# A Fourier mixing and expert kernel: the order of work from fixed slots to list scheduling over streams

## The chip, the cores and the metric

The kernel runs on one core of one Trainium2 chip. The metric is device time in microseconds (us) of the whole program. TensorE (PE) multiplies, VectorE (DVE) and ScalarE (ACT) move results out of PSUM and do elementwise work, GpSimd (POOL) issues indirect transfers (scatter and gather by row numbers), and SyncE (SP) issues all other transfers, in order, on one queue. Everything is in float32.

## The reference

Two blocks follow each other. The first filters 8 sequences of 2496 tokens with 256 channels in the frequency domain; the second sends each of the 19968 tokens to the one expert of 8 with the highest logit.

```
X = rfft(x, axis=1);  Y = X * (filt_r + 1j * filt_i);  y = irfft(Y, n=2496)     # x: 8 x 2496 x 256
logits = y @ w_gate;  e = argmax(logits);  gate = softmax(logits)[e]             # per token
out = gate * (relu(y @ w1[e]) @ w2[e])                                           # w1: 8 x 256 x 1024, w2: 8 x 1024 x 256
```

## The kernel before

**The transform.** 2496 = 39 x 64, so the Fourier transform and its inverse are four stages of products with small tables, batch by batch. Stage a (`stage_a`, line 336) multiplies x by a 117 x 117 table and stores z. Stage b (line 349) loads z with the other index along the partitions, multiplies by the tables `tbs`, and VectorE multiplies by the filter `ht`. Stage c (lines 371 and 373) goes back and stores u. Stage d (line 394) loads u, multiplies by `tds` and stores y. z, u and y are tensors in DRAM: their layout is turned on the way out and in. A batch goes in 6 chunks of up to 4 slices for stages a and d and in 5 chunks for b and c. After stage d, y is transposed (`turn_y`, line 407), multiplied by `w_gate` (`logits`, line 421) and turned back (`turn_logits`, line 432).

**The routing.** `route` finds each token's expert and its rank within the expert (two products, lines 468 and 469, called rank products below), and scatters token numbers and gates into a table in DRAM, sorted by expert: 22 indirect transfers per batch on POOL (line 510), 30 for the last batch. `tile_map` then makes tiles of 512, 256 or 128 rows of one expert, 65 in all: one of 256 rows after batch 0, one of 512 and five of 256 after batch 1, then only 512 until the last batch, which ends with 256 and 128.

**The experts.** For each tile `listed` loads its list of rows (line 596), `gather` fetches the rows of y (line 612), `weights` loads w1 and w2 of its expert (1 MB each, lines 631 and 627), `turn_x` transposes (line 639), `hidden` computes relu(x w1) (line 646, eight times two products), `result` multiplies by w2 (line 661), scales by the gate and scatters 128 rows to the output (line 667).

**What sets the order.** A planner in Python writes each engine's order out by hand. `slot(k)` mixes stages b and c of batch k, stage a of batch k+1 and stage d of batch k-1 by fixed places within a slot; `STEPS` is all slots one after the other. The loop at the end takes either the next step of `STEPS` or the next piece of expert work, by a credit that `share()` refills, and keeps a clock `now` of TensorE's work. A transform step may be placed as soon as its load has been put in SP's queue (`f[2] in ins`); it doesn't know when the load lands. `more_loads` fills one ring of 8 input buffers (`fin`, tag "in") in the order of the steps; a load of z or u must wait until the last store of its batch has been put in the queue. Stores are put in the queue two steps late by `move` and `flush`. `prefetch` puts list loads, gathers and weights in the queues as buffers allow. Results of stages a, c and d share five buffers (tag "st"), freed when their stores have landed. The tables are loaded between the steps of slot 0.

SP executes its queue in order: an instruction that waits holds up everything behind it.

```
    NIN = 8
    ...
        if may("list", 3):
            i = got["list"]
            listed(i)
            mark("list", max(now[0], rows_at[work[i][3]]) + 5.0)
    ...
            elif f and (not f[2] or f[2] in ins):
```

Of the kernel before, what the change touches and what calls it, by code (L numbers as in the profile page):

```python
# [133 lines left out]
def kernel(  # L134
# [37 lines left out]
    zd = [dram.tile([N2, N1, D], F32, tag=f"z{b % 2}", name="zd") for b in range(B)]  # L172
    ud = [dram.tile([N2, N1, D], F32, tag=f"u{b % 2}", name="ud") for b in range(B)]
# [44 lines left out]
    free = {"v": 0.0, "s": 0.0, "p": 0.0}  # L218
# [27 lines left out]
    def load_filters(c):  # L246
        f0, n = FH[c]
        nc.sync.dma_start(out=tbs[:, f0:f0 + n], in_=tb[:, f0:f0 + n])
        nc.sync.dma_start(out=ht[:, f0:f0 + n], in_=filt[:, f0:f0 + n, :])
        if c == 0:  # L250
            nc.sync.dma_start(out=ht[:, NF:], in_=filt[:, NF:, :])
            nc.sync.dma_start(out=tcs, in_=tcm)

    def load_rest():
        nc.sync.dma_start(out=tds, in_=td)
# [37 lines left out]
    NIN = 8  # L293

    moves, stored = [[], []], set()

    def move(o, i):
        moves[1].append(lambda: nc.sync.dma_start(out=o, in_=i))

    def mark(key):  # L300
        moves[1].append(lambda: stored.add(key))
# [6 lines left out]

    def fin(key):
        ins[key] = sb.tile([P, 4, D], F32, tag="in", name="fin", bufs=NIN)  # L310
        return ins[key]

    def load_x(b, c):
        i0, n = CH[c]
        nc.sync.dma_start(out=fin(("x", b, c))[:, :n], in_=x[b, :, i0:i0 + n, :])

    def load_z(b, c):
        f0, n = FH[c]
        z0 = 1 if f0 == 0 else 0
        zi = fin(("z", b, c))  # L320
        nc.sync.dma_start(out=zi[:HP, :n], in_=zd[b][:, f0:f0 + n, :])
        nc.sync.dma_start(out=zi[HP:, z0:n], in_=zd[b][:, NF - 1 + f0 + z0:NF - 1 + f0 + n, :])

    def load_u(b, c):
        i0, n = CH[c]
        ui = fin(("u", b, c))
        for r, m, v in columns(ud[b], i0, n):
            nc.sync.dma_start(out=ui[r, :m], in_=v)

    def stage_a(b, c):  # L330
        i0, n = CH[c]
        xt = ins.pop(("x", b, c))
        zo = sb.tile([TP, 4, D], F32, tag="st", name="zo", bufs=5)
# [4 lines left out]
        for r, m, v in columns(zd[b], i0, n):  # L338
            move(v, zo[r, :m])
# [3 lines left out]
    def stage_b(b, f):  # L343
# [16 lines left out]
        free["v"] = max(free["v"], now[0]) + 2.8  # L360

    def stage_c(b, f):
        ys = outs.pop(("y", b, f))
        j = f % 4
        if j == 0:
            outs["u", b] = sb.tile([P, 4, D], F32, tag="st", name="uo", bufs=5)
# [8 lines left out]
        if j == 2:  # L375
            f0 = f - 2
            z0 = 1 if f0 == 0 else 0
            move(ud[b][:, f0:f0 + 4, :], uo[:HP])
            move(ud[b][:, NF - 1 + f0 + z0:NF - 1 + f0 + 4, :], uo[HP:, z0:])
# [3 lines left out]
    def stage_d(b, c):  # L383
# [4 lines left out]
        yo = outs["o", b, c] = sb.tile([TP, 4, D], F32, tag="st", name="yo", bufs=5)  # L388
# [9 lines left out]
        for r, m, v in columns(ytok, i0, n):  # L398
            move(v, yo[r, :m])
# [39 lines left out]
    def route(b):  # L439
# [68 lines left out]
        rows_at[b] = pool(now[0] + 5.0, len(rows)) + 3.0  # L508
# [124 lines left out]
    def turn_x(i):  # L633
        n, xg = work[i][0], xgs.pop(i)
        xts[i] = moe.tile([P, DH, 4 * P], F32, tag="xT", name="xT")
# [17 lines left out]
    def result(i, j):  # L653
# [10 lines left out]
        pool(now[0], 1)  # L664
        either(D, lambda: nc.vector.tensor_scalar(ys, in0=p[:, :D], scalar1=gate, scalar2=None, op0=ALU.mult),  # L665
# [13 lines left out]
    def slot(k):  # L679

        steps, nch = [], len(CH)
        if k < B:
            for f in range(0, NF + 2, 2):
                at = f / (NF + 2)
                if f < NF:
                    steps.append((at, lambda f=f: stage_b(k, f), ("z", k, f // 4) if f % 4 == 0 else None, 0.85))
                if f >= 2:
                    steps.append((at + 0.01, lambda f=f: stage_c(k, f - 2), None, 0.85))
        if k + 1 < B:
            for c in range(nch):  # L690
                steps.append((0.7 * c / nch, lambda c=c: stage_a(k + 1, c), ("x", k + 1, c), 0.43 * CH[c][1]))
        if k > 0:
            for c in range(nch + 3):
                at = 0.2 + 0.8 * c / (nch + 3)
                if c < nch:
                    steps.append((at, lambda c=c: stage_d(k - 1, c), ("u", k - 1, c), 0.43 * CH[c][1]))
                if c >= 3 and c % 2:
                    steps.append((at + 0.01, lambda c=c: logits(k - 1, (c - 3) // 2), None, 0.9))
                if 1 <= c <= nch:
                    steps.append((at + 0.03, lambda c=c: turn_y(k - 1, c - 1), None, 0.22 * CH[c - 1][1]))  # L700
                if c >= 3 and c % 2:
                    steps.append((at + 0.04, lambda c=c: turn_logits(k - 1), None, 0.25))
            steps.append((2.0, lambda: begin_route(k - 1), None, 0.0))
        return sorted(steps, key=lambda step: step[0])

    STEPS = []
    for c in range(len(CH)):
        STEPS.append((0.0, lambda c=c: stage_a(0, c), ("x", 0, c), 0.43 * CH[c][1]))
        if c < len(FH):
            STEPS.append((0.0, lambda c=c: load_filters(c), None, 0.0))  # L710
    STEPS.append((0.0, load_rest, None, 0.0))
    SLOT = []
    for k in range(B + 1):
        steps = slot(k)
        SLOT.append(sum(step[3] for step in steps))
        STEPS += steps

    def begin_route(b):
        flush(True)
        sides.append(after(b))  # L720
        left_t[0] = SLOT[b + 2] if b + 2 <= B else 1.0


# [144 lines left out]
```

## Time and profile before

| | |
|---|---|
| median of 3 runs | 1713.04 us (1707.46 to 1716.94) |
| profiled execution, its own time | 1714.15 us |
| its span, first to last instruction | 1712.4 us |
| mean granted clock of TensorE | 0.960 |
| instructions | 20473 |
| bytes moved by DMA | 296.11 MB, mean 173 GB/s |
| DMA packets | 120962 |

Busy time by group of instructions (count, busy us, mean ns of one record; a float32 product shows as two records):

| group | count | busy us | mean ns |
|---|---|---|---|
| result, line 661, w2t | 2240 | 501.3 | 381 |
| hidden, line 646, all forms | 2080 | 589.5 | 436 |
| result, line 661, w2s | 368 | 83.2 | 379 |
| stage b, line 349, all forms | 320 | 92.3 | 412 |
| stage d, line 394, all forms | 352 | 92.1 | 403 |
| stage a, line 336 | 176 | 89.1 | 631 |
| stage c, line 373 | 144 | 79.1 | 633 |
| scatter to the table, line 510 (POOL) | 176 | 174.2 | 990 |
| scatter to the output, line 667 (POOL) | 163 | 163.2 | 1001 |
| gather, line 612 (POOL) | 163 | 157.6 | 967 |

How to read it: the span is one execution as the hardware profiler saw it; the medians are from runs of their own. Matmuls are pipelined and the profile models their ends, so the mean of one record is longer than the distance from one to the next. In a row by stretch the columns are the stretch, its length, the busy us of PE, PEld (weight loads), DVE, ACT and POOL with counts, the granted clock, the busy share of the 16 DMA engines and the GB/s moved. In a list of waits, "PE bank L432 <- ACT yt L232: 33.1, 2, 17.9" says that TensorE's line 432 waited for ScalarE's line 232, 33.1 us in total, twice, at most 17.9. In order of time the bracket at the end is the engine's idle time before the row and what ended it; SPq is SP's queue, and its rows are the issue of a transfer. Line 232 is `evac`, the helper for all copies out of PSUM; line 298 is `move`, for all stores.

### The profile page before, as it was taken

How to read it: one execution, taken by the hardware profiler on the slowest of the kernel's cores; microseconds unless marked ns; L12 is line 12 of the kernel's file. 1: busy time of each engine (PE TensorE's matmuls, PEld its weight loads, DVE VectorE, ACT ScalarE, POOL GpSimd, SP SyncE). 2: the span in 40 equal slices, each digit the busy share in tenths (PEclk: the TensorE clock that was granted, in tenths of full speed). 3: DMA queues.
4: the chain of work that ended last, by engine and by line, in shares of the span. 5: the costliest groups of instructions: out<-in, count | busy, mean ns of one | idle time of the engine just before them, and what ended most of it. 6: DMA issues, size and time to landing. Idle time of an engine off the chain costs nothing. (4 is left out here: it accounts for less than half of the span.)

```text
span 1712.4 us, 20473 instructions
## 1 busy us (share of the span) xinstructions
PE 1574.1 (92%) x6822; PEld 1123.0 (66%) x6822; DVE 561.3 (33%) x1355; ACT 321.6 (19%) x587; POOL 504.5 (29%) x526
## 2 busy tenths in 40 slices
PE   2888387898999999999999989999999999999997
PEld 1454245577857766666657657666666668889996
DVE  0647173354452214322252223231000003334442
ACT  1233131311232122222222212221212120000000
POOL 0002315024234311531234315374322222222221
PEclk7889688999999999999999999999999999999999
DMA  8988787658876354664365343405343435554551
GB/s 293 274 250 207 209 232 199 209 174 215 276 198 216 129 180 130 161 217 138 112 154 172 117 135 104 160 5 194 131 163 136 155 132 201 184 184 173 175 185 41
DMA packets 120962, 296.11 MB, mean 173 GB/s; under 512 B 32338, under 2 KB 73028, under 8 KB 105893
## 3 DMA queue, kind: packets, MB, share of 16 engines
q1 hardware_dynamic: 99322, 252.77, 48.4%
q0 software_dynamic: 21536, 42.03, 7.5%
q8 instruction: 56, 0.92, 0.2%
q14 instruction: 48, 0.39, 0.1%
HBM read 212.74 MB, written 82.88 MB: 173 GB/s over the span
## 5 line engine op out<-in xcount | busy, mean ns | idle before, releaser
L646 PE MATMUL bank<-xT,w1t 128*128 128x512 f32 (+2 forms) x2080 | 589.5, 436 | 6.7 <-DVE xT L232 5.0
L661 PE MATMUL bank<-w2t,hT 128*128 128x256 f32 x2240 | 501.3, 381 | 4.6 <-DVE hT L649 4.6
L646 PEld LDWEIGHTS bank<-xT,w1t 128*128 128x128 f32 x2080 | 340.8, 192 | 215.8 <-issue 188.3
L661 PEld LDWEIGHTS bank<-w2t,hT 128*128 128x128 f32 x2240 | 421.7, 191 | 71.0 <-issue 10.8
L667 POOL DMA_INDIRECT out_dram<-ys,idt x163 | 163.2, 1001 | 570.6 <-DVE ys L665 193.4
L510 POOL DMA_INDIRECT table<-pay,row x176 | 174.2, 990 | 318.9 <-DVE row L495 216.5
L612 POOL DMA_INDIRECT xg<-yd,idt x163 | 157.6, 967 | 306.4 <-PE bank L639 234.1
L665 DVE TENSOR_SCALAR ys<-bank,idt 128x256 f32<-128x256 f32 x151 | 73.0, 484 | 476.5 <-PE bank L661 431.3
L650 ACT ACTIVATE hT<-bank 128x512 f32<-128x512 f32 (+1 forms) x234 | 137.4, 587 | 476.1 <-PE bank L646 476.1
L649 DVE TENSOR_SCALAR hT<-bank 128x128 f32<-128x128 f32 (+1 forms) x286 | 96.9, 339 | 70.1 <-PE bank L646 68.1
L349 PE MATMUL bank<-fin,tbs 128*128 128x256 f32 (+1 forms) x320 | 92.3, 412 | 27.4 <-issue 26.3
L394 PE MATMUL bank<-fin,tds 117*117 117x256 f32 (+1 forms) x352 | 92.1, 403 | 17.2 <-DMA fin<-ud 16.6
L349 PEld LDWEIGHTS bank<-fin,tbs 128*128 128x128 f32 (+1 forms) x320 | 62.3, 206 | 59.7 <-issue 47.5
L394 PEld LDWEIGHTS bank<-fin,tds 117*117 117x117 f32 (+1 forms) x352 | 66.5, 193 | 49.0 <-issue 23.9
L336 PE MATMUL bank<-fin,tas 117*117 117x512 f32 x176 | 89.1, 631 | 6.3 <-DMA fin<-in_x_dram 5.8
L356 DVE TENSOR_TENSOR ys<-bank,ht 128x512 f32<-128x512 f32 x80 | 55.1, 688 | 117.7 <-PE bank L349 117.5
L373 PE MATMUL bank<-ys,tcs 128*128 128x512 f32 x144 | 79.1, 633 | 12.1 <-DVE ys L359 6.2
L232 ACT COPY xT<-bank 128x512 f32<-128x512 f32 (+2 forms) x69 | 29.4, 432 | 305.4 <-PE bank L639 201.4
L232 ACT COPY uo<-bank 128x512 f32<-128x512 f32 x80 | 46.9, 586 | 201.4 <-PE bank L373 120.0
L232 DVE COPY xT<-bank 128x512 f32<-128x512 f32 (+2 forms) x61 | 29.1, 477 | 165.2 <-PE bank L639 165.0
L661 PE MATMUL bank<-w2s,hT 128*128 x368 | 83.2, 379 | 0.0
L661 PEld LDWEIGHTS bank<-w2s,hT 128*128 128x128 f32 x368 | 68.1, 190 | 8.3
(103 smaller groups left out, 769.0 us busy)
## 6 DMA issues: line engine op xcount, KB each, us to landing
w1t<-in_moe_w_dram SPq DMA_DIRECT2D x65, 1024.0 KB
w2t<-in_moe_w_dram SPq DMA_DIRECT2D x42, 1024.0 KB
fin<-in_x_dram SPq DMA_DIRECT2D x40, 512.0 KB
zd<-zo SPq DMA_DIRECT2D x120, 156.0 KB
fin<-ud SPq DMA_DIRECT2D x120, 156.0 KB
yd<-yo SPq DMA_DIRECT2D x120, 156.0 KB
fin<-zd SPq DMA_DIRECT2D x72, 256.0 KB
ud<-uo SPq DMA_DIRECT2D x72, 256.0 KB
```

Source lines behind the costliest of these rows:

```text
L232: either(n, lambda: nc.vector.tensor_copy(o, i), lambda: nc.scalar.copy(out=o, in_=i))
L336: mm(p[:TP, :], lhsT=tas, rhs=xt[:TP, j:j + 2, :], start=True, stop=True)
L349: mm(p[:, i * D:(i + 1) * D], lhsT=tbs[:k, f + i, :], rhs=zi[:k, j + i, :], start=True, stop=True)
L373: mm(p, lhsT=tcs[:, 1, :], rhs=ys, start=True, stop=True)
L394: mm(p[:TP, i * D:(i + 1) * D], lhsT=tds[:k, i0 + j + i, :], rhs=ui[:k, j + i, :], start=True, stop=True)
L510: sc = nc.gpsimd.indirect_dma_start(out=table, out_offset=bass.IndirectOffsetOnAxis(ap=at, axis=0), in_=what, in_offset=None,)
L612: nc.gpsimd.indirect_dma_start(out=xgs[i][:, j], out_offset=None, in_=yd[0:rows, :], in_offset=bass.IndirectOffsetOnAxis(ap=idt[i].bitcast ...
L646: mm(p[:, :m], lhsT=w1t[i][:, dh, k * P:(k + 1) * P], rhs=xts[i][:, dh, :m], start=(dh == 0), stop=(dh == DH - 1))
L649: either(m, lambda: nc.vector.tensor_scalar_max(hT[:, :m], p[:, :m], 0.0), lambda: nc.scalar.activation(hT[:, :m], p[:, :m], AF.Relu))
L650: lambda: nc.scalar.activation(hT[:, :m], p[:, :m], AF.Relu))
L661: mm(p[:, :D], lhsT=hs[i][k][:, j * P:(j + 1) * P], rhs=w2, start=(k == 0), stop=(k == FT - 1))
L667: nc.gpsimd.indirect_dma_start(out=out, out_offset=bass.IndirectOffsetOnAxis(ap=ids.bitcast(U32)[:, j, 0:1], axis=0), in_=ys, in_offset=No ...
```

## The change

The order by slots goes. There are now four streams, each with its own order: A (stage a), X (stages b and c), Y (stage d, transposes, logits, routing) and the experts. `transform()` takes the first step of Y, X or A, in this priority, whose input has landed by the planner's clock; A may run one batch ahead of X. The planner keeps a time for the transfers (`free["d"]`, at 240 or 380 GB/s by kind) and `ready` times of loads and of VectorE's results. A list load is put in SP's queue only when the planner's clock has passed the batch's scatters. Input buffers are per stream (2 for x, 3 for z, 3 for u), z and u have a DRAM tensor for each batch, "st" has six buffers, the transposed expert input one. The tables come with the z loads of batch 0, each part ahead of its chunk. `share()` counts what is left of the streams up to the next routing. What is computed stays the same.

```
-    zd = [dram.tile([N2, N1, D], F32, tag=f"z{b % 2}", name="zd") for b in range(B)]
+    zd = [dram.tile([N2, N1, D], F32, tag=f"z{b}", name="zd") for b in range(B)]
...
+    ROW, ROWS = 0.24e6, 0.38e6
+    def dma(size, rate):
+        free["d"] = max(free["d"], now[0]) + size / rate
+        return free["d"] + 2.5
...  load_filters: the filters' last part by chunk
+        half, f1 = divmod(f0, NF // 2)
+        rows = slice(half * HP, (half + 1) * HP)
+        nh = min(n, NF // 2 - f1)
+        nc.sync.dma_start(out=ht[rows, NF + f1:NF + f1 + nh], in_=filt[rows, NF + f1:NF + f1 + nh, :])
+        if nh < n:
+            nc.sync.dma_start(out=ht[HP:, NF:NF + n - nh], in_=filt[HP:, NF:NF + n - nh, :])
         if c == 0:
-            nc.sync.dma_start(out=ht[:, NF:], in_=filt[:, NF:, :])
             nc.sync.dma_start(out=tcs, in_=tcm)
...
-    NIN = 8
+    NIN = {"x": 2, "z": 3, "u": 3}
...
     def mark(key):
-        moves[1].append(lambda: stored.add(key))
+        def store():
+            stored[key] = free["d"] + 2.0
+        moves[1].append(store)
...  load_z
+        if b == 0:
+            load_filters(c)
+            if c == 2:
+                load_rest()
...  load_x, load_z, load_u return when the load lands
+        return dma(P * n * D * 4, ROWS)        # x and z
+        return dma(TP * n * D * 4, ROW)        # u
...
-        zo = sb.tile([TP, 4, D], F32, tag="st", name="zo", bufs=5)
+        zo = sb.tile([TP, 4, D], F32, tag="st", name="zo", bufs=6)
...
-        rows_at[b] = pool(now[0] + 5.0, len(rows)) + 3.0
+        rows_at[b] = pool(now[0] + 1.0, len(rows)) + 3.0
...
-        xts[i] = moe.tile([P, DH, 4 * P], F32, tag="xT", name="xT")
+        xts[i] = moe.tile([P, DH, 4 * P], F32, tag="xT", name="xT", bufs=1)
...  slot() and STEPS go; A, X and Y hold (batch, step, cost, input)
+    def more_loads():
+        for kind, load, todo, source in loads:
+            while todo and sum(key[0] == kind for key in ins) < NIN[kind]:
+                b, c = todo[0]
+                if source and stored.get((source, b), 1e9) > now[0]:
+                    break
+                todo.pop(0)
+                ready[kind, b, c] = load(b, c)
+    def transform():
+        for stream in (Y, X, A):
+            if stream and (not stream[0][3] or ready.get(stream[0][3], 1e9) <= now[0]):
+                if stream is A and stream[0][0] > (X[0][0] + 1 if X else B):
+                    continue
+                return stream
+        return None
...  prefetch
-        if may("list", 3):
-            i = got["list"]
-            listed(i)
-            mark("list", max(now[0], rows_at[work[i][3]]) + 5.0)
+        if may("list", 3) and rows_at[work[got["list"]][3]] <= now[0]:
+            listed(got["list"])
+            mark("list", now[0] + 5.0)
...  share
-        return min(4.0, max(0.3, (known - RESERVE) / max(left_t[0], 1.0)))
+        return min(4.0, max(0.3, (known - (45.0 if b < B - 1 else 80.0)) / max(left, 1.0)))
...  the loop
+            f = transform()
+            asked = e and when.get(e[2], 1e9) <= now[0]
+            if asked and (credit > 0.0 or not f):
                 e[0]()
                 now[0] += e[1]
-                credit -= e[1]
+                credit = max(credit - e[1], -20.0)
...
+            elif f:
+                step = f.pop(0)
+                step[1]()
+                now[0] += step[2]
+                credit = min(credit + share() * step[2], 20.0)
             else:
-                now[0] += 1.0
+                now[0] += 0.5
```

## The prediction

> **What bounds the kernel now.** I read the page's busy lines and slices first, then busy time by stretch, then TensorE's waits in the first 323 us, then SP's own waits, then the order of time around one long wait.
>
> ```profile
> PE 1574.1 (92%) x6822; PEld 1123.0 (66%) x6822; DVE 561.3 (33%) x1355; ACT 321.6 (19%) x587; POOL 504.5 (29%) x526
> ...
> PEclk7889688999999999999999999999999999999999
> DMA  8988787658876354664365343405343435554551
> ```
> ```profile
> 0.00:250.00 250.00, 166.76 (x600) 96.58 (x600) 119.92 (x233) 64.28 (x117) 28.53 (x43) 0.83 0.84 244
> 250.00:323.00 73.00, 51.24 (x244) 36.42 (x244) 34.64 (x88) 14.39 (x28) 26.83 (x28) 0.86 0.75 211
> 323.00:420.00 97.00, 90.09 (x373) 66.69 (x367) 39.65 (x101) 18.24 (x35) 35.68 (x36) 0.96 0.69 185
> 420.00:1167.00 747.00, 732.84 (x2999) 496.85 (x2998) 237.13 (x572) 169.48 (x298) 268.07 (x273) 0.99 0.53 157
> 1167.00:1712.00 545.00, 533.12 (x2616) 426.43 (x2614) 129.93 (x364) 55.16 (x110) 145.34 (x148) 0.99 0.44 155
> ```
> Columns: stretch, length, busy us of PE, PEld, DVE, ACT, POOL, granted clock, DMA share, GB/s. From 323 us on TensorE is the bound: it idles 7 + 14 + 12 us in 1389. Before 323 it idles 105 of 323 us and runs at 0.83 to 0.86 of its clock while the DMA share is 0.84: this stretch is bound by transfers.
>
> ```profile
> PE bank L432 <- ACT yt L232: 33.1, 2, 17.9
> PE bank L349 <- issue: 26.3, 1, 26.3
> PE bank L394 <- DMA fin<-ud: 10.8, 3, 6.5
> ...
> SPq L596 <- DMA table<-pay,row: 17.8, 2, 10.8
> ```
> ```profile
> 181.92 0.47 SPq L322 DMA_DIRECT2D fin<-zd  x1
> 190.96 0.38 SPq L596 DMA_DIRECT2D idt<-table  x1
> 192.15 0.82 SPq L631 DMA_DIRECT2D w1t<-in_moe_w_dram  x1
> 193.76 0.34 SPq L627 DMA_DIRECT2D w2t<-in_moe_w_dram  x1
> 194.21 1.31 SPq L298 DMA_DIRECT2D zd<-zo  x3
> ...
> 210.65 0.69 DVE L232 COPY yo<-bank 117x512 f32<-117x512 f32 x1 [20.08 <-DMA zd<-zo]
> ...
> 211.79 0.53 PE L432 MATMUL bank<-ident,ls 128*117 128x128 f32 x1 [17.90 <-ACT yt L232]
> ```
> The third block is TensorE's waits up to 323 us (total, times, longest) with one of SP's; the last is order of time. SP has one in-order queue. At 182 us it reaches the list load of batch 0, which needs all 22 scatters of that batch, and stands 8.6 us (a second time 265.4 to 277.6: 12.2). Behind it wait the stores that free the "st" buffers, so VectorE and ScalarE cannot evacuate, and TensorE stops for 17.9 and 15.2 us. The 26.3 us wait is the first z load behind 6.5 MB of tables.
>
> **The unit of the sum.** I add up TensorE's work at full clock. A product of 512 columns takes two records of 0.43 us (32 records of L646 fill 13.73 us), one of 256 columns 0.43 us in all (64 records of L661: 13.82 us), eight transposes of y 0.80, eight logit products 0.93. All work of the program is then 1518 us. It is the same in both programs; only its order differs. The landmark is the start of the first 512-row expert tile, from which on TensorE has expert work to fill gaps with. Before, it starts at 323.2 us (the transposes of line 639). By the built order, 183 us of work stand before it: 55 products of stage a (47.3), 80 of b (34.4), 43 of c (33.5), 66 of d (28.4), transposes and logits 20.8, the 256-row tile and the small rest 18.4. So 140 us are lost by then. From there to the last product's end at 1701.6 are 1378.4 us for 1335.3 of work: 43 lost (22.6 idle by the stretches above, the rest clock and rounding). After it 10.8 us of last store and end. 183 + 140 + 1335 + 43 + 11 = 1712, the span. The profiled execution took 1714.15, the median is 1713.04: I subtract 1.1 at the end.
>
> **The change, part by part.**
>
> *List scheduling.* In the changed program's order the same landmark has 54, 72, 38 and 66 products of stages a to d before it, 175 us of work. Rank products of batch 1 come after 122 us of work instead of 128, of batch 2 after 165 instead of 230, since batches no longer go in lockstep slots. But transfers bound this stretch, so I count bytes in SP's queue. Up to the landmark tile's w1 load: 65.6 MB before, 67.2 MB after. The order alone does not lighten the start: fewer z and x loads of later batches, but the same tables and stores.
>
> *The list load's gate.* `listed` is now put in the queue only when the planner's clock has passed the last scatter (22 x 1.3 us planned, 1.29 measured start to start). The two blocks, 20.8 us of a standing queue, go. In the early stretch the planner's rates (240 and 380 GB/s) are above the 244 measured, so real time runs behind the planner and the scatters have longer than planned: the gate should hold. What is late next: the 2 MB of weights themselves, which still go ahead of the stores (7 us at 290 GB/s).
>
> *When the landmark comes.* Two workings. (a) The w1 load of the landmark was issued at 278.8 us; less 20.8 of standing queue 258; 1.6 MB more at 260 GB/s, 6; landing 5 (the u load issued at 88.98 us was used at 94.16): 269. (b) 67.2 MB at 260 GB/s (the share-1 rate is 244/0.84 = 290; I take a share of 0.90, between 0.84 and the 0.97 to 1.04 of the best 10 us pieces), 258, and 5: 263. I take 266. Bounds: 67.2/0.244 + 5 = 280, and at a share of 0.97, 67.2/0.281 + 5 = 244.
>
> *Tables with the z loads.* The 6.5 MB of tables move from between the stores of batch 0 to behind them. The filters' last quarter comes in pieces, which adds 5 DMAs to SP's queue (about 0.45 us each, L251's issue), 2 us on a queue that is waiting for bytes anyway: 0. What was late before (z0 at 43.5 us) is late still, for table bytes come directly ahead of each z chunk. It is inside the bytes above.
>
> *Own z and u tensors per batch, own buffers per stream.* Removes waits on old loads and stores (SP's waits on zd and ud before a load are 1 to 3 us each). Eight shared input buffers become 2 for x, 3 for z, 3 for u: look-ahead gets shorter. After the landmark some 70 loads (30 u, 22 z, 18 x) remain, and each is issued only when the step that used its buffer is done. The planner gives a u load 0.479 MB/240 + 2.5 = 4.5 us; the trace shows 5.2 in the busy start. z: 3.9 planned, 3.75 shown (39.76 to 43.51). If every u, z and x load were late by 0.7 us, that is 49 us. Against it: before, steps were placed as soon as their load was issued, with no landing time, and after 323 us TensorE waited for inputs from ud once, 5.8 us. Expert products stand between most steps. I take 5 us. Bounds: -20 (all 22.6 us of late idle gone but what the rank products cause) and +49.
> [...] The measurement decides on the latency; how much of it is covered only the run tells.
>
> *st 5 to 6, xT 2 to 1.* One more store buffer loosens the evacuations (gain inside the above). With one xT the transposes of tile i+1 still come after all products that read xT of tile i on the same engine: 0; where they cannot go early, the evacuation is exposed once, at most the 5.0 us that the first tile shows (PE L646 after DVE xT L232).
>
> *The end.* The last batch's first tile comes 66 us of work after its rank products (10.4 + 13.8 + 0.9 + 3 x 13.8). Before, from those (1109.83) to the list load (1154.71) took 44.9; 3.6 for the list (190.96 to 194.60), 4.8 for four gathers, 4.3 for landing (first x load: 1.32 to 5.58): 57.6. Covered by 9 us: I take 0. If it slips: up to 10 us.
>
> Sum: 266 + 1343 (1518 - 175) + 43 + 5 + 10.8 = 1667.8, plus 1.75 around the span, less 1.1: **1668 us**.
>
> **Rivals.**
> *A. The queue runs nearly full* and the late idle goes too. Landmark 244, late term -15 instead of +5: 1668 - 22 - 20 = 1626. For: pieces of 10 us at a share of 1.0. Against: the pieces between them at 0.65, where SP waits for evacuations; that dependency stays.
> *B. The gate does not hold or bytes bind harder.* Landmark 280 and 0.2 us per load: 1668 + 14 + 9 = 1691. If SP blocks as before, the 33.1 us of TensorE's wait come back: 1701. For: 1.6 MB more in the queue than before.
> *C. Slower: short look-ahead.* Every load after the landmark becomes a bubble on the in-order TensorE. From 1663 without bubbles, 70 loads x 0.71 us reach 1713; at 1 us each, 1733. For: 2 x buffers, and the 5.2 us above. Against: the one late wait before, and that DMA share is 0.53 there.
>
> **How the numbers follow.** Half a per cent, 8.6 us, is about what can be told from no change. Forecast 0.52 (1645 to 1690), A 0.14, B 0.17 (three quarters of it faster, the rest no change), C 0.17 (0.03 of it within half a per cent). Faster 0.52 + 0.14 + 0.13 = 0.79; same 0.04 + 0.03 = 0.07; slower 0.14. The range 1626 to 1722 leaves out the best of A and most of C. If the change is faster at all, 1626 to 1701.
>
> **What would show it.** The first 512-row tile near 266 us (A: 244, B: 280); no SP wait on table scatters before it and no TensorE wait over 10 us on ScalarE's yt; the DMA share to that point near 0.90. In the later stretch, TensorE's idle near 25 us with waits on fin<-ud, fin<-zd or fin<-in_x under 10 us in sum (C: 50 or more, in many waits of about 1 us). Rank products of the last batch to its first tile without a gap over 5 us. The forecast falls if the queue stands for evacuations instead of lists, or if TensorE's order was planned for transfers faster than they are.

## The result and the profile after

The changed kernel takes 1762.31 us (median of 4 runs, 1751.32 to 1765.67) against 1713.78 for the kernel before: a ratio of 1.0277, 95% interval 1.0223 to 1.033. It is slower; the prediction said 1668. The profiled execution has a span of 1760.4 us and took 1762.14. The runs below were taken in groups, each beside the kernel before, which took 1711 to 1718 us in three groups, 1793 in that of e5 to e8 and 1796 in that of e17 and e18, so between groups only ratios are compared.

The page of the changed kernel, busy line and slices:

```profile
PE 1596.1 (91%) x6822; PEld 1127.9 (64%) x6822; DVE 568.6 (32%) x1369; ACT 315.6 (18%) x573; POOL 505.6 (29%) x526
...
PE   5587877499899999989999999999988999999997
...
DMA  7998869548535842374483643473243435555551
```

Busy time by stretch, columns as before (stretch, length, PE, PEld, DVE, ACT, POOL, granted clock, DMA share, GB/s). The second stretch ends at the landmark of the prediction, the start of the first 512-row expert tile:

```profile
0.00:250.00 250.00, 173.13 (x594) 97.82 (x595) 122.96 (x273) 56.28 (x102) 35.36 (x50) 0.84 0.87 233
250.00:333.00 83.00, 46.97 (x230) 31.96 (x228) 36.14 (x88) 14.00 (x25) 39.42 (x41) 0.82 0.81 213
333.00:420.00 87.00, 85.55 (x339) 63.65 (x340) 25.26 (x47) 15.07 (x30) 18.22 (x19) 0.95 0.50 154
420.00:1167.00 747.00, 718.29 (x2829) 478.47 (x2829) 228.79 (x493) 166.78 (x292) 238.89 (x242) 0.98 0.52 158
1167.00:1760.00 593.00, 572.19 (x2835) 455.99 (x2833) 155.50 (x469) 63.49 (x125) 173.74 (x176) 0.98 0.43 149
```

The landmark comes at 333 us: ten later than before, 67 later than predicted. In the 250 to 333 stretch TensorE works 47 of 83 us. The late stretches are worse too: 28.7 us idle in the fourth where the kernel before had 14.2.

TensorE's waits over the whole span (total, times, longest):

```profile
PE bank L669 <- DMA xg<-yd,idt: 48.7, 16, 30.0
PE bank L365 <- DMA fin<-in_x_dram: 26.2, 10, 7.0
PE bank L378 <- DMA fin<-zd: 25.9, 6, 8.8
...
PE bank L676 <- DVE xT L239: 10.1, 1, 10.1
...
PE bank L424 <- DMA fin<-ud: 4.0, 5, 1.8
```

The 33.1 us of waits on ScalarE's yt, which the change was to remove, are gone. New are one wait of 30.0 us for gathered rows (`turn_x`, now line 669), one of 10.1 us for a copy, and many smaller ones for x (line 365), z (line 378) and gathered rows. Where the 30 us come from shows in order of time, by the queues of SP and POOL and by TensorE:

```profile
290.15 0.38 SPq L626 DMA_DIRECT2D idt<-table  x1
291.33 0.37 SPq L661 DMA_DIRECT2D w1t<-in_moe_w_dram  x1
...
273.20 1.02 POOL L698 DMA_INDIRECT out_dram<-ys,idt  x1 [6.04 <-issue]
299.08 1.01 POOL L540 DMA_INDIRECT table<-pay,row  x1 [24.86 <-DVE row L525]
...
327.00 0.90 POOL L540 DMA_INDIRECT table<-pay,row  x1 [0.30 <-issue]
328.45 0.98 POOL L642 DMA_INDIRECT xg<-yd,idt  x1 [0.55 <-DMA table<-pay,row]
...
301.99 1.02 PE L403 MATMUL bank<-ys,tcs 128*128 128x512 f32 x2
333.05 0.75 PE L669 MATMUL bank<-ident,xg 128*128 128x128 f32 x2 [30.04 <-DMA xg<-yd,idt]
```

The tile's list is loaded at 290. POOL is idle from 274 to 299, but the next instruction in its queue is the first of batch 2's 22 scatters (line 540), and it waits 24.86 us for its row numbers. Then all 22 go, one each 1.29 us, and only at 328.45 the first gather (line 642). The tile comes next in TensorE's written order, so TensorE stands from 303 on.

The 10.1 us stand at the last batch, in order of time on VectorE and TensorE:

```profile
1311.54 0.48 DVE L696 TENSOR_SCALAR ys<-bank,idt 128x256 f32<-128x256 f32 x1 [25.64 <-DMA out_dram<-ys,idt]
...
1324.60 0.68 DVE L239 COPY xT<-bank 128x512 f32<-128x512 f32 x1
...
1314.15 1.13 PE L676 MATMUL bank<-xT,w1t 128*128 128x512 f32 x2 [0.28 <-ACT xT L239]
1325.33 16.04 PE L676 MATMUL bank<-xT,w1t 128*128 128x512 f32 x30 [10.05 <-DVE xT L239]
```

POOL's queue in the same place, the last scatter to the table and the first two to the output:

```profile
1294.34 0.97 POOL L540 DMA_INDIRECT table<-fill,pad  x1 [0.30 <-issue]
...
1305.58 1.03 POOL L698 DMA_INDIRECT out_dram<-ys,idt  x1 [0.30 <-issue]
...
1312.25 1.03 POOL L698 DMA_INDIRECT out_dram<-ys,idt  x1 [4.38 <-DVE ys L696]
```

The 30 scatters of the last batch hold POOL's queue until 1295; then it stands 6.46 us at a gather, and only at 1305.58 does the next scatter to the output go. Until then the four ys buffers stay full, and VectorE stands 25.64 us on a free one. After that the outputs follow 3 to 7 us apart, each with one ys result of VectorE behind it. The copy that TensorE needs is the next but three on VectorE.

Here the stall cost somewhat more than its length. The same place by stretches of 5 us (the columns as above; the clock is the one after POOL's):

```profile
1310.00:1315.00 5.00, 4.72 (x24) 3.46 (x22) 0.48 (x1) 0.59 (x1) 1.03 (x1) 1.00 1.04 416
1315.00:1320.00 5.00, 0.28 (x1) 0.00 (x0) 0.48 (x1) 0.00 (x0) 1.01 (x1) 0.75 0.76 309
1320.00:1325.00 5.00, 0.00 (x0) 0.00 (x0) 1.28 (x3) 0.00 (x0) 2.74 (x3) 0.50 0.21 67
1325.00:1330.00 5.00, 4.67 (x6) 2.09 (x7) 0.28 (x1) 0.60 (x1) 3.11 (x4) 0.50 0.38 116
1330.00:1335.00 5.00, 5.00 (x11) 2.15 (x11) 0.00 (x0) 1.59 (x3) 1.53 (x2) 0.88 0.07 26
```

After the stall TensorE still has half its clock for some 6 us (to about 1331), which by an estimate from these rows costs 3 us: the stall of 10.05 us is worth some 13. By an estimate from the same rows, the mean of 0.75 puts the fall from 1.00 to 0.50 some 2 to 2.5 us after the last product (1315.3), and the mean of 0.88 puts the return some 6 us after the work (1325.3).

By the prediction's unit (TensorE's work at full clock, 1518 us in all) the loss up to the landmark and behind it is:

| kernel | span | landmark | work before it | lost before it | lost after it |
|---|---|---|---|---|---|
| before | 1712.4 | 323.2 | 182.9 | 140 | 54 |
| after | 1760.4 | 333.1 | 175.3 | 158 | 84 |
| e1, gather first | 1731.0 | 298.9 | 175.3 | 124 | 89 |
| e2, gate alone | 1706.9 | 304.0 | 182.9 | 121 | 68 |
| e4, 4/2/2 buffers | 1697.1 | 330.7 | 194.2 | 136 | 43 |
| e9, e1 once more | 1728.8 | 296.4 | 175.3 | 121 | 90 |
| e10, 8 ys, 5 st | 1728.0 | 314.5 | 175.3 | 139 | 71 |
| e11, 2 xT, 5 st | 1746.3 | 313.3 | 175.3 | 138 | 90 |
| e13, 3/3/2 buffers | 1675.4 | 300.8 | 183.9 | 117 | 40 |
| e14, 2/3/2 buffers | 1716.6 | 358.1 | 194.2 | 164 | 35 |

Lost before is the landmark less the work before it; lost after is the span less the landmark less the rest of the work. "After it" holds the 10.8 us of the last stores. Of the 48 us between before and after, 18 lie before the landmark and 30 behind it.

### The profile page after: what moved, and what is told of

It reads as the page before. It is cut to its first block, busy times and chain, and to the rows that moved or that the text cites. A ratio compares the mean times of both kernels' runs of the same rounds, so it can differ in the third digit from the quotient of the medians.

```text
span 1760.4 us, 20409 instructions
## 1 busy us (share of the span) xinstructions
PE 1596.1 (91%) x6822; PEld 1127.9 (64%) x6822; DVE 568.6 (32%) x1369; ACT 315.6 (18%) x573; POOL 505.6 (29%) x526
## 5 line engine op out<-in xcount | busy, mean ns | idle before, releaser
L676 PE MATMUL bank<-xT,w1t 128*128 128x512 f32 (+2 forms) x2080 | 599.4, 441 | 14.1 <-DVE xT L239 10.1
L696 DVE TENSOR_SCALAR ys<-bank,idt 128x256 f32<-128x256 f32 x142 | 68.6, 483 | 466.2 <-PE bank L691 424.7
L365 PE MATMUL bank<-fin,tas 117*117 117x512 f32 x176 | 100.5, 704 | 26.2 <-DMA fin<-in_x_dram 26.2
L669 PE MATMUL bank<-ident,xg 128*128 128x128 f32 x326 | 53.4, 291 | 48.7 <-DMA xg<-yd,idt 48.7
L239 DVE COPY xT<-bank 128x512 f32<-128x512 f32 (+2 forms) x63 | 30.2, 479 | 191.9 <-PE bank L669 191.6
L424 PE MATMUL bank<-fin,tds 117*117 117x256 f32 (+1 forms) x352 | 85.7, 382 | 5.4 <-DMA fin<-ud 4.0
L669 PEld LDWEIGHTS bank<-ident,xg 128*128 128x128 f32 x326 | 41.4, 148 | 67.8 <-issue 47.5
L365 PEld LDWEIGHTS bank<-fin,tas 117*117 117x117 f32 x176 | 36.3, 214 | 73.6 <-issue 61.6
```

The lines of the kernel that those rows point to most:

```text
L365: mm(p[:TP, :], lhsT=tas, rhs=xt[:TP, j:j + 2, :], start=True, stop=True)
L424: mm(p[:TP, i * D:(i + 1) * D], lhsT=tds[:k, i0 + j + i, :], rhs=ui[:k, j + i, :], start=True, stop=True)
L669: nc.tensor.transpose(pt[:, j, :], xg[:, j, dh * P:(dh + 1) * P], ident)
L676: mm(p[:, :m], lhsT=w1t[i][:, dh, k * P:(k + 1) * P], rhs=xts[i][:, dh, :m], start=(dh == 0), stop=(dh == DH - 1))
```

## The experiments

Line numbers in an experiment's rows are those of its own kernel. Theory: POOL's queue works in order, so the gather stood behind scatters (30 us); two x buffers slow the start; the tail's output buffers cost 10 us and a half-clock stretch. Rivals: bytes bind the start, the rows come late by themselves, or what one place gains another takes back.

### e1 and e9: the gather ahead of the scatters

```
+            if b == HELD:                     # HELD = 2: kept back until the next gather() is in the queue
+                held.append(lambda at=at, what=what: scatter(at, what))
...
-            gather(i)
+            name = gather(i)
+            if len(rows_at) > HELD:
+                let_go(name)                  # each held scatter is ordered behind that gather
```

> The changed kernel with one thing moved: the 22 table scatters of batch 2 are queued on GpSimd behind the gather of the first 512-row expert tile and not ahead of it; the orders of TensorE and of the load queue are as in the changed kernel. Theory (GpSimd's queue works in order, and the gather stood behind scatters that waited 24.86 us for their row numbers and then took 28 us): the list of that tile is issued at 290, its rows can be gathered from 295 and land by about 303, and TensorE's work before it ends at 303.0; the wait of 30.04 us at that tile falls to 0 to 4 us, the tile starts at 302 to 307 and the kernel takes 1732 to 1740. Rival one (the rows come late for the transfer's own sake, behind other traffic): the wait stays above 20 us and the time within 1755 to 1768. Rival two (what is gained at the tile is lost again later, because the late part is bound by something else): the tile starts near 305 but the time stays above 1750.

Measured: 1731.65 us, ratio 1.0134 (1.0102 to 1.0167). POOL and TensorE in order of time:

```profile
290.33 0.99 POOL L656 DMA_INDIRECT xg<-yd,idt  x1 [20.14 <-DMA idt<-table]
...
309.19 1.02 POOL L548 DMA_INDIRECT table<-pay,row  x1 [0.31 <-issue]
...
298.85 0.59 PE L684 MATMUL bank<-ident,xg 128*128 128x128 f32 x2
```

The gather runs as soon as its list has landed, and the tile starts at 298.9 without a wait, somewhat ahead of the expected 302 to 307. The time falls by 30.7 us, as much as the wait was long, but the two kernels were timed in different groups: by ratio (1.0277 and 1.0134) it is 25 us, and against e3, which has the same wait (30.2 us) and ran beside e1, it is 21. The first theory holds; both rivals fall. The loss before the landmark is now 124, less than before the change; the loss behind it hardly moves (84 and 89).

> The kernel with the gather put first once more, to stand beside the next three on one chip. Theory and rivals as before: a ratio of 1.008 to 1.019 to the kernel before, a stall of 10 to 12 us at the last batch's second dense tile (TensorE waiting for VectorE's xT copy).

The same kernel in another group: 1731.51 us, ratio 1.0104 (1.0048 to 1.016).

### e2: the gate alone, in the kernel before

```
-        if may("list", 3):
+        if may("list", 3) and rows_at[work[got["list"]][3]] <= now[0]:
```

> The kernel before with one part of the change alone: a list is loaded only when the planner reckons its scatters done. Theory (of the prediction): the load queue no longer stands on lists ahead of landmark tile and the 33.1 us for which TensorE waited on token transposes there go for the most part; first 512-row tile at 295 to 305 in place of 323, time 1688 to 1700. Rival (the queue stood where the transfers were behind anyway, or the gated list is then late for the tile itself): the waits move to gathered rows or to loads of x, z and u, the first 512-row tile stays within 315 to 330, time 1705 to 1725.

Measured: 1710.37 us, ratio 0.9999 (0.9962 to 1.0036). TensorE in order of time:

```profile
240.09 3.73 PE L394 MATMUL bank<-fin,tds 117*117 117x256 f32 x8 [11.56 <-DMA fin<-ud]
...
303.97 1.09 PE L639 MATMUL bank<-ident,xg 128*128 128x128 f32 x8
```

The waits on yt vanish and the landmark comes at 304, as expected; but 11.6 us of a u load and others take part of their place, the next tile (327.6) is only 10.7 us earlier than before (338.3), and the span 5.5 us shorter. In the time of the runs nothing is left. So the 20.8 us of a standing load queue, which the prediction took as the gain in its working (a), were worth at most 6 us in the kernel before.

### e12: the changed kernel without the gate

```
-        if may("list", 3) and rows_at[work[got["list"]][3]] <= now[0]:
-            listed(got["list"])
-            mark("list", now[0] + 5.0)
+        if may("list", 3):
+            i = got["list"]
+            listed(i)
+            mark("list", max(now[0], rows_at[work[i][3]]) + 5.0)
```

> The kernel with the gather put first, and without the gate on the lists: a list is loaded as soon as a buffer is free, as before. The planner's order shifts a little with it. Theory (the gate makes the first list of each batch late, and the 17 us of waits on gathered rows after 350 us with their half-clock stretches are its price): these waits fall below 6 us and the ratio is 0.006 to 0.014 lower. Rival (without the gate the load queue stands on scatters, as in the kernel before with 8.6 and 12.2 us): TensorE waits on token transposes or loads come back, ratio the same within 0.003 or higher.

Measured: 1781.12 us, ratio 1.0383 (1.0325 to 1.0442), 50 us above e9. One line of SP's waits and TensorE's two largest, in order of time:

```profile
SPq L640 <- DMA table<-pay,row: 149.4, 16, 32.0
```
```profile
192.97 3.73 PE L365 MATMUL bank<-fin,tas 117*117 117x512 f32 x4 [27.45 <-DMA fin<-in_x_dram]
...
304.85 5.50 PE L378 MATMUL bank<-fin,tbs 64*128 64x256 f32 x12 [32.20 <-DMA fin<-zd]
```

The theory (the gate is the price of the late waits on rows) is right that these waits go (0.6 us is left behind 340 us), but without the gate SP stands 149.4 us on scatters, where it stands 51.8 in e9. The waits also go with the gate kept, in e13 and e14 (at most 0.5 us), so it is not the gate alone that makes them. In the plan of the four streams the gate is needed; in the old plan it was nearly free either way. (The planner's order shifts with it, so the 50 us are not the gate's alone.)

### e5, e10 and e11: the tail's output buffers, st and xT

```
-        ys = moe.tile([P, D], F32, tag="ys", name="ys", bufs=4)
+        ys = moe.tile([P, D], F32, tag="ys", name="ys", bufs=8)      # e5, e10
-        xts[i] = moe.tile([P, DH, 4 * P], F32, tag="xT", name="xT", bufs=1)
+        xts[i] = moe.tile([P, DH, 4 * P], F32, tag="xT", name="xT", bufs=2)      # e11
-        ... tag="st", name="zo", bufs=6)          # and uo, yo
+        ... tag="st", name="zo", bufs=5)          # e5, e10, e11, for the space
```

> The kernel of the run with the gather put first (1731.65), with 8 output tiles ys in place of 4; the space is taken from st, 5 in place of 6. The orders of TensorE and of the load queue stay the same. Theory (the stall of 11.2 us near 1297 comes from the 30 scatters of the last batch, which hold GpSimd's queue for about 50 us while outputs pile up: with four ys buffers VectorE stands on a free one, and the xT copy behind it is late): with eight buffers the stall is under 3 us, the half-clock stretch of 13.7 us behind it goes too, and the time is 1712 to 1720. Rival one (the xT copy waits for the gathered rows themselves): the stall stays at 8 to 12 us, time 1728 to 1736. Rival two (the sixth st buffer matters): waits of stage outputs early in the run eat the gain, time 1722 to 1735.

Measured: ratio 1.0012 (0.9977 to 1.0047), in a group in which the kernel before took 1792.68. The stall at the last batch is gone in its trace, but the ratio can't be set against e1's. The same kernel beside e9:

> 8 ys buffers in place of 4 and 5 st in place of 6, beside the kernel with the gather put first on the same chip (the earlier try ran where every kernel was 4 to 5 per cent slower and TensorE often stood without a releaser, so its 1.0012 can't be set against 1.0134). Theory (four output buffers behind 30 scatters make VectorE, and with it the xT copy, late): the stall of 10 to 12 us at the last batch falls under 3 us and the ratio is 0.007 to 0.012 lower. Rival (the xT copy waits for something else): stall and ratio stay within 0.003.

> The kernel with the gather put first, with 2 xT buffers in place of 1 and 5 st in place of 6; orders unchanged. The prediction put the single xT buffer at 0 to 5.0 us. Theory (0): the ratio stays within 0.003 of the kernel with the gather put first, and the stall at the last batch stays, since its copy is late and not its buffer. Rival (the single buffer delays the next tile's transposes): the waits on gathered rows of 1 to 5 us at the first tile of each batch and the stall shrink, ratio 0.004 to 0.010 lower.

Measured: e10 1734.63 us (1.0114, 1.006 to 1.0168), e11 1746.82 us (1.018, 1.0124 to 1.0235), e9 1731.51. TensorE at the last batch in order of time, e9 first, then e10:

```profile
1294.56 15.25 PE L691 MATMUL bank<-xT,w1t 128*128 128x512 f32 x30 [11.22 <-DVE xT L239]
```
```profile
1293.89 14.00 PE L691 MATMUL bank<-xT,w1t 128*128 128x512 f32 x32 [0.28 <-ACT xT L239]
```

With 8 buffers the stall is gone; with 4 and two xT (e11) a stall of 9.7 us is there. So the mechanism holds in this plan: full output buffers, and not xT. (In e4, e13 and e14, where the plan differs, four ys buffers are enough: no wait on an xT copy there is over 2 us.) Its size: e10 is 12.2 us below e11, and loses 19 us less behind the landmark than e9 and e11 (71 against 90). Not all of this is the stall: against e9, waits on xT copies are 10.3 us less (5.4 against 15.7), small waits on gathered rows 4.6 less (13.9 against 18.5), and the granted clock from 1150 to 1350 is 1.00 against 0.97, by an estimate another 6 us (0.03 of 200). But e10 isn't faster than e9. The loss before the landmark grew from 121 to 139, and in e11 too. What both change is the sixth st buffer, so it seems worth 15 to 18 us at the start; no run gave it up alone. The ratio that e10's expectation named (0.007 to 0.012 lower) didn't come; the second rival of e5's expectation did.

### e3: shared z and u tensors

```
-    zd = [dram.tile([N2, N1, D], F32, tag=f"z{b}", name="zd") for b in range(B)]
+    zd = [dram.tile([N2, N1, D], F32, tag=f"z{b % 2}", name="zd") for b in range(B)]        # ud the same
```

> The changed kernel with the two DRAM tensors shared between batches again, as before (b modulo 2); all orders of work stay those of the changed kernel. Theory (a store into a shared tensor finds its readers long done): same time, 1757 to 1768. Rival (the sharing cost what the prediction put at 5 us): 1764 to 1772, with waits of z and u stores on reads of two batches earlier in the load queue.

Measured: 1752.82 us, ratio 1.0244 (1.0217 to 1.0271), within the interval of the changed kernel's, though 4 us below both expected ranges. No gain of own tensors shows.

### e4, e13, e14, e17 and e18: the input buffers

```
-    NIN = {"x": 2, "z": 3, "u": 3}
+    NIN = {"x": 4, "z": 2, "u": 2}      # e4;  x 3, z 3, u 2: e13, e17;  2, 3, 2: e14;  3, 3, 3: e18
```

> The changed kernel with 4 input buffers for x, 2 for z and 2 for u in place of 2, 3 and 3. The planner's order follows, and with it the gather of the first 512-row tile comes ahead of batch 2's scatters. Theory (the start is slow because only two loads of x are ahead: 210 GB/s over the first 50 us against 293 in the kernel before): the first 50 us move 260 to 300 GB/s, the list of the first 512-row tile is issued at 265 to 278 and the tile starts at 278 to 290; time 1710 to 1730. Rival (the start is slow because the tables came to stand beside the z loads, or for the order of the stores): the first 512-row tile starts at 300 to 308 as with the gather put first alone, time 1732 to 1745.

Measured: 1696.44 us, ratio 0.9911 (0.9879 to 0.9942). Faster than the kernel before, by 0.9 per cent, and below the expected 1710 to 1730. The first 50 us move 265 GB/s, as expected, but the landmark comes at 330.7: the plan now puts 194 us of work ahead of it, so its time alone is no measure where the plan moves, and the losses of the table are. Those before it are 136. Waits on z grew to 49.7 us. The larger part of the gain is behind the landmark (43 lost).

So x was separated, with e1's order of the gather in both:

> The kernel with the gather put first, with 3, 3 and 2 input buffers for x, z and u (2, 3 and 3 there). Beside it runs one with 2, 3 and 2, so the pair differs by the third x buffer alone (and what the planner makes of it). Theory (two x buffers make the start slow): waits on x up to 150 us fall from about 20 to below 10 us, the first 50 us move over 240 GB/s, and the time is 10 to 25 us below the one with 2, 3 and 2. Rival (the start is bound by bytes; waits on x turn into waits on z): within 6 us of it.

> The kernel with the gather put first, with 2, 3 and 2 input buffers: the control for the third x buffer. If the third u buffer counts for nothing, its time is that with 2, 3 and 3 (1731.5) within 6 us; if u needs it, waits on ud grow by 10 us or more.

Measured: e13 1673.74 us, ratio 0.976 (0.9731 to 0.9788); e14 1714.15 us, 1.0002 (0.9977 to 1.0026). The third x buffer, and the plan that goes with it, are worth 40 us, where 10 to 25 were expected. First stretch and TensorE's waits on x, e14 and then e13:

```profile
0.00:50.00 50.00, 27.38 (x42) 10.45 (x42) 8.15 (x18) 6.55 (x10) 1.72 (x16) 0.81 0.74 214
```
```profile
PE bank L365 <- DMA fin<-in_x_dram: 53.8, 18, 19.6
```
```profile
0.00:50.00 50.00, 28.37 (x50) 10.68 (x50) 11.30 (x23) 7.72 (x12) 1.72 (x16) 0.89 0.86 262
```
```profile
PE bank L365 <- DMA fin<-in_x_dram: 14.0, 8, 5.3
```

214 against 262 GB/s, 53.8 against 14.0 us of waits on x. The expected sign in the first 150 us is only half right: waits on x fall from 21.6 to 12.9 there, waits on z rise from 19.4 to 23.9; the larger part of the gain comes between 150 and 350, where e14's longest wait (19.6) lies. e14 also shows that the third u buffer isn't free of effect: with two the ratio is 0.010 below e9's, and the loss behind the landmark is 35 and not 90, though waits on ud grow from 5.1 to 16.6 us. The plan comes out differently there; which of its differences does it was not separated.

> The changed kernel with 3, 3 and 2 input buffers and nothing else: the scatters of batch 2 are not held, but with these buffers the first dense tile's gather comes ahead of them by itself, and 11 of the 22 stand ahead of the next tile's gather. Theory (the third x buffer carries the gain, the hold only matters where scatters stand ahead of a gather that is needed): within 8 us of the run with the hold, 1668 to 1684. Rival (the hold carries a part): 1690 to 1705, with a wait of over 10 us on gathered rows near 320.

> The kernel with the gather put first, with 3, 3 and 3 input buffers, and 5 st in place of 6 for the space. Against the kernel with 2, 3, 3 and 5 st (1734.6 with 8 ys, 1746.8 with 4), theory (the third x buffer is worth 30 to 40 us whatever u has): 1695 to 1715. Rival (it was the buffers for u, 2 in place of 3, that changed the plan for the better): 1735 to 1750.

The kernel before took 1795.77 us beside both, so only ratios count. e17, the changed kernel with this one line changed, has 0.9758 (0.9704 to 0.9813), the same as e13: with these buffers the first dense tile's gather is ahead of the scatters by itself and the hold isn't needed. e18 has 0.9897 (0.9841 to 0.9953), against 1.0114 for e10 and 1.018 for e11 with two x buffers: 0.02 to 0.03 for the third x buffer also where u has three, though between two groups. (By ratio 0.976 and 0.99 of 1713 are 1672 and 1695, each as its theory had it.) e13 is the best version that was run: 40 us below the kernel before, 89 below the changed one.

### e6, e7, e8, e15 and e16: the place of the tables, and the third z buffer

```
-        if b == 0:                      # in load_z
-            load_filters(c)
-            if c == 2:
-                load_rest()
...
+                stage_a(b, c)
+                if b == 0 and c < len(FH):
+                    load_filters(c)
+                if b == 0 and c == len(CH) - 1:
+                    load_rest()
```

> The kernel with 4, 2 and 2 input buffers (1696.44) with the tables of the transform loaded between the first stage's steps as before, and not with batch 0's z loads; TensorE's order is the same. Theory (of the prediction: the bytes are the same and only the place moves, cost 0): the z waits of 11.6, 14.4, 4.1 and 3.2 us at 47 to 87 become one wait of 22 to 28 us at the first z; time 1690 to 1702. Rival (tables beside the z loads delay every z load and cost 10 us or more of the start): time 1678 to 1688, and the waits up to 100 us sum to under 25 us in place of 45.

> The changed kernel with 4, 3 and 2 input buffers for x, z and u (space from st, 5 in place of 6), so a third z buffer beside the run with 4, 2 and 2. Theory (with two z buffers the next z load starts too late: waits for z of 5.3 us at 166 and 12.1 us at 191): these two waits fall below 5 us together and the time is 1678 to 1690. Rival (the early part is bound by bytes, so the wait only moves to another load): waits for loads up to 330 us stay at 60 to 80 us in all, time 1692 to 1702.

> The same 4, 3 and 2 buffers with the tables loaded early as before; TensorE's order is that of the run with 4, 3 and 2. If tables beside the z loads cost nothing, the time is that of that run within 5 us; if they cost the start 10 us, it is 8 to 14 us lower. Against the kernel before: 1672 to 1692, faster.

All three are of e5's group: ratios 0.9807 (0.9739 to 0.9875), 0.9849 (0.98 to 0.9897), 0.9825 (0.9757 to 0.9894). The three intervals overlap: neither the third z buffer (e6 against e8, which also gives up an st buffer) nor the place of the tables (e7 against e8) shows. In e7 the two late z waits fall from 17.3 to 0.9 us, as its theory says, but no gain in time can be told.

> The changed kernel with 4, 2 and 2 input buffers once more, beside the same with early tables: a ratio of 0.986 to 0.996 to the kernel before.

> 4, 2 and 2 input buffers with the tables loaded between the first stage's steps, as before. If the place of the tables costs nothing (the prediction), within 4 us of the one with 4, 2 and 2 buffers on the same chip; if tables beside the z loads cost the start 10 us, ratio 0.978 to 0.986.

e15: 1688.32 us, 0.9851 (0.9828 to 0.9875). e16: 1697.05 us, 0.9915 (0.9886 to 0.9945). The medians say that early tables cost 9 us, the two profiled spans are equal (1688.0 and 1687.9), and e7 and e8 show no difference. So within a group the place of the tables is worth something between nothing and 9 us, in favour of the change.

e15 is e4's kernel, e16 is e6's and e10 is e5's, and their ratios differ between groups by more than the intervals allow: 0.9911 and 0.9851, 0.9807 and 0.9915, 1.0012 and 1.0114. Between groups, then, a difference in ratio of about 0.01 (17 us) proves nothing, and that between e14 and e9 is no larger.

## Why the prediction was wrong

**The landmark, predicted at 266, was 333.** Working (a) started from the w1 load issued at 278.8, less 20.8, plus 6, plus 5. It followed SP's queue alone. The step that failed is that the tile starts when its weights have come. POOL's queue has no term in the working: the tile's rows must be gathered, and the gather is in that queue, where the change moves the routing of batch 2 ahead of it (the prediction itself noted that batch 2's rank products come after 165 us of work and not 230). The gather was issued at 328.45, 37 us after the weights, and TensorE stood 30.04 us for it. With the order of that queue alone put right the tile starts at 298.9 (e1), 34 us earlier, and 21 to 31 us of the time go. The rest is 33 us: the w1 load went out at 291.3 and not at 264, since 67.2 MB by then are 231 GB/s and not the 260 of working (b). The input buffers have a part in this. SP's waits over the whole span, loads of x, z and u that wait for TensorE to be done with a buffer:

```profile
SPq L337 <- PE bank L365: 57.7, 12, 15.8
...
SPq L348 <- PE bank L378: 48.5, 5, 20.7
...
SPq L356 <- PE bank L424: 37.1, 10, 7.0
```

In the kernel before all such rows together are 13 us. Before the x load issued at 257.65 the queue stood 12.0 us on its buffer, and the stores that follow from 258.27, the list at 290.15 and the weights at 291.33 were behind it; e13 against e14 shows 40 us for one more x buffer (where the row for x is 35.3 and 38.9, so its length is not the whole of it). The prediction named the two x buffers under its slower rival, but priced them only behind the landmark.

**The list gate.** "The gate should hold" was right only in part. TensorE's waits on ScalarE's yt are gone, but one of the prediction's signs, no SP wait on table scatters ahead of the landmark, failed: there is one of 8.4 us (the list issued at 212.69), and over the whole span they are still half of the 69.1 us (10 times) in the kernel before:

```profile
SPq L626 <- DMA table<-pay,row: 36.0, 7, 10.4
```

Of the two planner's rates only 380 GB/s is above the measured 244; 240 is not, so the reason given for the gate was half right. That its 20.8 us would come off the landmark nearly holds in the kernel before, where the gate alone moves it by 19 us (e2). That the time would follow does not: the sum keeps the loss behind the landmark fixed, and there it grew from 54 to 68 us.

**Tables with the z loads, 0,** is right within 9 us in favour of the change. **Own z and u tensors**: no gain shows (e3), where the prediction had them in one term with the buffers.

**Short look-ahead, 5 us, bounds -20 and +49.** The mechanism of rival C, a bubble at each load, didn't come: behind 336 us the waits on fin<-ud are 0.5 us. The late loss grew for other reasons, from 54 to 84 by the table where the prediction had 59: 17.8 us of waits on gathered rows, 10.1 at the last batch, and a lower clock around them: 0.74 from 455 to 460, 0.50 from 755 to 760, 0.68 from 930 to 935, 0.63 from 1150 to 1155, 0.50 from 1320 to 1330. At one of these places, in e1, the rows wait for POOL once more (POOL in order of time, then TensorE):

```profile
705.03 0.98 POOL L713 DMA_INDIRECT out_dram<-ys,idt  x1 [7.26 <-issue]
710.70 0.98 POOL L713 DMA_INDIRECT out_dram<-ys,idt  x1 [4.68 <-issue]
711.99 0.99 POOL L656 DMA_INDIRECT xg<-yd,idt  x1 [0.30 <-issue]
...
716.90 0.30 PE L684 MATMUL bank<-ident,xg 128*128 128x128 f32 x1 [1.25 <-DMA xg<-yd,idt]
```

The list had been issued at 694.34, after SP stood 10.4 us on the scatters; the gather then stands behind outputs that wait for their products. Elsewhere the list itself is late: in e1 one is issued at 1106.98, and its gather follows at 1109.35 with 0.50 us of idle time before it. This reading of the small late waits is from the rows. The waits go without the gate (e12) and with other buffers (e13, e14), but these runs change the whole plan, so the cause is not separated.

**st 5 to 6, xT 2 to 1: 0, at most 5.0.** The stall that this bound was for is not xT's. But st looks mis-sized: without the sixth buffer 15 to 18 us more are lost before the landmark (e1 and e9 against e10 and e11, which share no other change).

**The end: "I take 0. If it slips: up to 10 us".** It slipped by 10.1 us, and with the half-clock stretch by some 13. The 57.6 us chain was counted from the rank products to the rows, and these came in time; what was late was VectorE behind full ys buffers, which the chain didn't hold.

Of the rivals, B had the bytes right in direction (280 as its landmark) but neither the size nor the main cause, and C had the slower result by a mechanism that didn't come. No rival named POOL. The forecast's own sentence "the forecast falls if the queue stands for evacuations instead of lists" looked at SP's queue alone.

## What to carry to other kernels

Where an order of work is changed, read the order of every in-order queue that the moved steps feed, the indirect transfers' too: here a scatter that waited 24.86 us for its row numbers held up the gather behind it, and 22 short scatters held it up for 28.8 us more. A planner that counts an engine's time but leaves that engine's order to another scheduler has not planned it: the engines whose order this kernel writes out are TensorE, VectorE, ScalarE and SyncE, and not POOL. When buffers are split by stream, give the stream that starts the program enough of them: here one line (x from 2 to 3, u from 3 to 2) decided between 1.03 and 0.976.

## What the runs showed of the hardware

After TensorE's wait of 10.1 us at the last batch the clock stayed at 0.50 for some 6 us, together a loss of some 13 us by the estimate above; after the wait of 30.04 us that ended at 333.05 it was 0.50 from 335 to 340 and 0.87 from 340 to 345. The 22 scatters of batch 2 followed each other every 1.29 us on POOL and held its queue for 28.8 us (299.08 to 327.90). Two small sizes that weigh more than expected: one 0.5 MB x buffer 40 us with the plan it brings, one st buffer 15 to 18 us, as far as two runs that share its loss show.

In the two groups in which the kernel before took 1792.68 and 1795.77 us, 4.6 to 4.8 per cent more than the 1713.44 beside e13, TensorE's waits have rows without a releaser. Of e17, while e13 has one such row of 1.6 us:

```profile
PE bank L669 <- issue: 17.4, 5, 8.7
PE bank L691 <- issue: 14.6, 14, 2.1
```

What they are the profile doesn't say, and it stays open. The chip's number doesn't settle it: e13 and e17 are both recorded on chip 1.
